# Loads of v and r behind the first inverse's operand, and a later planned start of the step that uses the inverse's result

## The chip, the core and the metric

The kernel runs on one core of a Trainium2 chip, as one program. The metric is device time in microseconds (us), the median of several runs. TensorE (PE), VectorE (DVE), ScalarE (ACT), GpSimd (POOL) and SyncE (SP) each work through their own instructions in program order. An instruction that waits holds up all that stand behind it on its engine. DMAs are issued from SP and, at a few places, from ACT, and an issue takes its turn in that engine's order too.

## The reference

A linear-attention recurrence over 768 steps, for 4 batches and 8 heads, then two feed-forward layers on the result:

```python
batch, n_heads, seq, head_dim = (4, 8, 768, 40)
for t in range(S):
    y[:, :, t] = np.einsum('bhd,bhde->bhe', rt, state)
    Sa = np.einsum('bhde,bhe->bhd', state, at)
    state_decay = state * wt[:, :, None, :] - np.einsum('bhd,bhe->bhde', Sa, bt)
    state = state_decay + np.einsum('bhd,bhe->bhde', vt, kt)
...
x = attn_out.transpose(0, 2, 1, 3).reshape(B * S, H * D)   # 3072 x 320
h = np.maximum(x @ w_in, 0.0); x = h * h @ w_out            # 320 -> 2048 -> 320
silu = g * (1.0 / (1.0 + np.exp(-g)))                       # g = x @ w_gate
out = silu * (x @ w_val) @ w_out                            # 320 -> 1536 -> 320
```

## The kernel before

**Chunks.** The 768 steps are cut into chunks of 32 (C). A unit is one chunk of two batches with all 8 heads. There are 48 units (NS), and units 2I and 2I+1 make a pair; 24 pairs follow each other in the recurrence, one waiting for the state of the last.

**Steps of a unit,** with the letter that the text uses and the line of the PE work: `e_stage` loads a, b, k, w (tile wakb, or room for two early units), scans the decays (DT) and forms AB and KB; x (L809) makes the 32x32 triangular matrix L of each head and stores it to DRAM (xi_d). For a window of 4 units, `inverse` loads the diagonal 16x16 blocks (tile xi, "the inverse's operand"), eliminates in 15 steps of two instructions each on DVE (L839, L842), and sends the result through DRAM (p_d<-xi, then p1t<-p_d). v (L868) needs p1t, p (L875) completes the inverse. Then the recurrence of a pair: u (L961, L967) needs v's values (tile TV) and the state, s (L980) applies the inverse to u, t (L1006) makes the new state. z, c, y (L1036, L1045, L1064) make the output and need the loads RB (v and r in another layout) and RH (r). The first feed-forward layer (L466, L471, tiles w1h, w1l, o1h, o1l, gh, gl; "MoE1" in the text) starts when units 0 to 3 have their y and runs between the attention's steps; its float64 weights (tile cx) are converted on ACT, DVE and POOL as they come in. Matmuls on the identity (L1299, "fillers") are put where the plan sees PE idle; their results are not used.

**What sets the order.** No order is written by hand. Every operation is handed to a planner (class `Plan`) with its engines' costs, what it reads and writes, and a due time. The planner plays the program through with these costs and issues each engine's instructions in the order that comes out. On the chip that order is fixed, and each instruction waits for what it really needs. `lag` is added to the planned arrival of what comes from a DMA:

```python
o.ready[e] = max(o.ready[e], p.done + (self.HOP[p.eng][e] + (o.lag if p.eng == SP or o.tag == "sq" else 0.0) if p.eng else 0.0))
```

**What the change touches.** `inverse` (keys of the load of xi), `stage` and the v step in `beside`, the loads of TV in `chain` and of RB and RH in `slot`. These loads may go on SP or, for the first units, on ACT (last argument of `load`). Their source lists were empty, so they could be issued as soon as their tile was free.

## Time and profile before

| what | value |
|---|---|
| three runs, median (lowest to highest) | 1197.45 us (1188.45 to 1198.04) |
| the profiled execution: its time, its span | 1193.31 us, 1191.5 us |
| PE busy | 1120.7 us, 94% |
| DVE, ACT, POOL busy | 642.9, 551.0, 97.5 us |
[...]
| y of the last unit starts | 736 us |

The first 740 us hold the attention with MoE1 between its steps, the rest of MoE1 and the second feed-forward layer follow. A row of the timeline is: start, duration, engine (with q: the engine's queue, which issues a DMA), line, operation, out<-in, shape, count, and in brackets how long the engine had been idle before it and what ended that.

### The profile page before, as it was taken

What the parts mean: (1) busy time and instruction counts of PE and PEld (TensorE: products, weight loads), DVE (VectorE), ACT (ScalarE), POOL (GpSimd) and SP (SyncE); (2) the same over time, 40 slices, a digit from 0 to 9 for tenths busy, and PEclk for the clock granted to TensorE, in tenths of its full rate; (3) what the DMA queues carried; (4) which work ended last, traced back from release to release, by engine and by line L of the source; (5) the groups of instructions that cost most, each with busy time, mean ns of one, the idle gap of its engine ahead of it and who ended that gap; (6) DMA issues with size and microseconds to landing.
All of it is one profiled execution on the core that took longest, in us unless ns stands there. A gap on an engine that the chain in (4) does not pass through costs nothing.

```text
span 1191.5 us, 43044 instructions
## 1 busy us (share of the span) xinstructions
PE 1120.7 (94%) x18634; PEld 1015.9 (85%) x18634; DVE 642.9 (54%) x1548; ACT 551.0 (46%) x1295; POOL 97.5 (8%) x122
## 2 busy tenths in 40 slices
PE   6688889999999998999999999999999999999997
PEld 5677778888989897889898899988888888888886
DVE  4776866757648573856464432455334343434433
ACT  6455876445546563655454454654223222222221
POOL 0211431101101111110000000000000000000000
PEclk9788988988999998999999999999999999999998
DMA  5754756455556564654443322432101010100000
GB/s 137 177 138 125 181 145 173 121 139 153 146 153 191 137 172 128 170 125 105 113 99 90 68 60 67 140 98 75 36 7 28 16 27 23 27 23 1 23 1 26
DMA packets 204695, 114.98 MB, mean 96 GB/s; under 512 B 104784, under 2 KB 203984, under 8 KB 204496
## 3 DMA queue, kind: packets, MB, share of 16 engines
q1 hardware_dynamic: 200867, 110.31, 36.1%
q8 instruction: 148, 2.42, 0.9%
q10 hardware_dynamic: 3629, 1.83, 0.6%
q14 instruction: 51, 0.42, 0.1%
HBM read 88.35 MB, written 23.72 MB: 94 GB/s over the span
## 4 chain that ended last, share of the span: by engine, by line
PE 69%; DMA 7%; DVE 3%; SPq 3%; issue 2%; ACT 1%; DVEq 0%; ACTq 0%
PE ps L466 32%; PE ps L471 11%; PE ps L1490 10%; SPq L730 3%; PE ps L1064 2%; PE ps L1045 2%; DMA ws<-f_moe_w_val 2%; DMA p1t<-p_d 1%; PE ps L1036 1%; PE ps L1006 1%; PE ps L967 1%; PE ps L980 1%; PE ps L868 1%; PE ps L1079 1%; PE ps L809 1%
## 5 line engine op out<-in xcount | busy, mean ns | idle before, releaser
L1482 DVE TENSOR_TENSOR gr<-ps,gr 128x512 f32<-128x512 f32 x144 | 99.5, 692 | 168.6 <-PE ps L466 85.8
L1158 ACT ACTIVATE ps<-ps 128x512 f32<-128x512 f32 x192 | 111.8, 582 | 97.6 <-PE ps L466 93.2
L471 PE MATMUL ps<-o1h,gh 128*128 128x320 f32 x384 | 132.8, 346 | 1.5 <-ACT gh L441 1.4
L441 ACT CAST gh<-gr 128x512 fp32r<-128x512 f32 x72 | 44.6, 620 | 175.7 <-DVE gr L1482 175.3
L471 PE MATMUL ps<-o1h,gl 128*128 128x320 f32 x384 | 122.8, 320 | 2.5 <-DVE gl L415 2.5
L471 PE MATMUL ps<-o1l,gh 128*128 128x320 f32 x384 | 121.5, 317 | 0.0
L466 PE MATMUL ps<-xh,w1h 128*128 128x256 f32 x384 | 115.6, 301 | 2.3 <-ACT xh L441 2.3
L466 PE MATMUL ps<-xl,w1h 128*128 128x256 f32 x384 | 109.6, 285 | 1.7 <-DVE xl L1107 1.0
L466 PE MATMUL ps<-xh,w1l 128*128 128x256 f32 x384 | 108.8, 283 | 0.3 <-DVE w1l L1239 0.3
L1490 PE MATMUL ps<-o2l,gh 128*128 128x320 f32 x288 | 88.7, 308 | 0.2 <-DVE o2l L1406 0.2
L1490 PE MATMUL ps<-o2h,gl 128*128 128x320 f32 x288 | 88.7, 308 | 0.1
L1490 PE MATMUL ps<-o2h,gh 128*128 128x320 f32 x288 | 88.7, 308 | 0.0
L415 DVE TENSOR_TENSOR gl<-ps,gh 128x512 fp32r<-128x512 f32 x96 | 65.6, 683 | 34.3 <-ACT gh L441 33.8
L1479 ACT ACTIVATE gr<-ps 128x512 f32<-128x512 f32 x72 | 43.1, 598 | 82.0 <-PE ps L466 80.3
L471 PEld LDWEIGHTS ps<-o1h,gh 128*128 128x128 f32 x384 | 75.1, 195 | 6.0 <-ACT gh L441 2.2
L471 PEld LDWEIGHTS ps<-o1h,gl 128*128 128x128 f32 x384 | 74.9, 195 | 5.8 <-DVE gl L415 5.5
L466 PEld LDWEIGHTS ps<-xh,w1h 128*128 128x128 f32 x384 | 74.1, 193 | 4.1 <-ACT xh L441 2.5
L466 PEld LDWEIGHTS ps<-xl,w1h 128*128 128x128 f32 x384 | 74.3, 193 | 2.6 <-DVE xl L1107 1.8
L471 PEld LDWEIGHTS ps<-o1l,gh 128*128 128x128 f32 x384 | 75.3, 196 | 0.1
L1139 DVE TENSOR_TENSOR gl<-gr,gh 128x512 fp32r<-128x512 f32 x72 | 49.8, 692 | 46.7 <-ACT gh L441 46.7
L466 PEld LDWEIGHTS ps<-xh,w1l 128*128 128x128 f32 x384 | 74.1, 193 | 0.5 <-DVE w1l L1239 0.5
L1299 PE MATMUL ps<-ident 128*128 128x256 f32 x296 | 51.7, 330 | 19.7 <-DVE w1l L1239 7.3
(171 smaller groups left out, 2725.2 us busy)
## 6 DMA issues: line engine op xcount, KB each, us to landing
wakb<-in_wakb_dram SPq DMA_DIRECT2D x44, 312.0 KB
RB<-in_vr_e_dram SPq DMA_DIRECT2D x45, 208.0 KB
RH<-in_r_e_dram SPq DMA_DIRECT2D x89, 80.0 KB
cx<-in_moe_w_out_dram SPq DMA_DIRECT2D x21, 320.0 KB
wakb<-in_wakb_dram SPq DMA_DIRECT2D x44, 110.5 KB
room<-xt_d SPq DMA_DIRECT2D x36, 128.0 KB
xt_d<-yb SPq DMA_DIRECT2D x24, 160.0 KB
x_d<-room SPq DMA_DIRECT2D x24, 160.0 KB
```

What stands on the lines that cost most here:

```text
L415: nc.vector.tensor_sub(dst, full, hi.bitcast(F32))
L441: nc.scalar.copy(dst, src) if e == ACT else eng[e].tensor_copy(dst, src)
L466: nc.tensor.matmul(ps, w[:, c], x, start=(i == 0), stop=(i == len(seq_) - 1))
L471: nc.tensor.matmul(acc[t][:, :DM], g[:, half, ts], w[:, f, :], start=(f == 0 and i == 0), stop=(f == nf - 1 and i == 2),)
L730: o = att(cost, lambda e: queues[e].dma_start(dst(), src()), r, w, due=due, dma=dma, tag="dma")
L1045: nc.tensor.matmul(v[64 * p:64 * p + 64, jh, u], RW[:, 4 * jh + 2 * u + p], RB[:, :, C * s:C * s + C], start=True, stop=True)
L1139: op({POOL: t_pool(512), DVE: t_dve(512)}, lambda e: eng[e].tensor_sub(gl[n], two["gr"][n], gh[n].bitcast(F32)), (("gr", n), ("gh", n)), ( ...
L1158: op({ACT: 0.478}, lambda e, f=f: nc.scalar.activation(P1[b], P1[b], f), (), (("p", b),), due=due, tag="relu")
L1299: nc.tensor.matmul(PS[:, b, 0:256].rearrange("p (a b) -> p a b", a=2), warm, warm[:, None, :].to_broadcast([128, 2, 128]), start=True, sto ...
L1479: op({ACT: 0.478}, lambda e: nc.scalar.activation(both(two["gr"]), two["pg"][b], AF.Sigmoid), (("pg", b),), (("gr", n),), tag="sig", **kw)
L1482: op({DVE: 0.602}, lambda e, q=q: nc.vector.tensor_mul(both(two["gr"]), two[q][b], both(two["gr"])), ((q, b),), (("gr", n),), tag="u" + q, ...
L1490: nc.tensor.matmul(ACC2[t][:, :DM], x[n][:, t // 2, c], y[:, f, :], start=(f == 0 and i == 0), stop=(f == nf - 1 and i == 2))
```

## The change

Three edits. (1) The load of xi gets a key ("xil", window, half), and for the first `BEHIND` = 4 units the loads of TV, RB and RH read this key of window 0: they are issued only when the first inverse's operand has landed. (2) v gets `lag` = 4.0: the plan takes v as ready 4 us later after its DMA than before. (3) RH loses the gap of 2 elements between its halves, so that its load is one row of 512 elements a partition instead of two of 256.

```diff
+LATE_V = 4.0
+BEHIND = 4
...
-    RH = ap_.tile([EPAD, 2, row], F32, name="RH")
+    RH = ap_.tile([EPAD, 2, 8 * C], F32, name="RH")
...
+    def behind(i):
+
+        return [("xil", 0, r) for r in range(2)] if i < BEHIND else ()
...
-        o = att({PE: cost}, lambda e: mm(tag), r, (tag,), due=due, take=n, tag=tag, mode=mode, act=act)
+        o = att({PE: cost}, lambda e: mm(tag), r, (tag,), due=due, take=n, tag=tag, mode=mode, act=act, lag=lag)
...
-                 [("xid", w % 2, o, p) for o in range(ns) for p in range(2)], (kx[r],), due - 1, 0.8, 0.7)
+                 [("xid", w % 2, o, p) for o in range(ns) for p in range(2)], (kx[r], ("xil", w, r)), due - 1, 0.8, 0.7)
...
-              ({ACT: 0.25}, lambda e, tag: copy(e, VT[:, :, :, 0:HC], view(tag)), ("vtz",), ("vt",)), mode="32x32", act=220)
+              ({ACT: 0.25}, lambda e, tag: copy(e, VT[:, :, :, 0:HC], view(tag)), ("vtz",), ("vt",)), mode="32x32", act=220, lag=LATE_V)
...
-                         lambda p=p, jh=jh, vsrc=vsrc: vsrc[p, jh], (), (("Tv", b, u, p, jh),), due - 0.7, 0.12, 0.62, I < SIDE)
+                         lambda p=p, jh=jh, vsrc=vsrc: vsrc[p, jh], behind(2 * I), (("Tv", b, u, p, jh),), due - 0.7, 0.12, 0.62, I < SIDE)
...
-            load(lambda p=p: RH[64 * p:64 * p + D, :, 0:8 * C], lambda: a["r_e"][data(i)].rearrange("d q s t -> d q (s t)"), (), (("Rr", p),), due + 0.3, 0.23, 0.0, i < 2 * SIDE)
+            load(lambda p=p: RH[64 * p:64 * p + D].rearrange("d q t -> d (q t)"), lambda: a["r_e"][data(i)].rearrange("d q s t -> d (q s t)"), behind(i), (("Rr", p),), due + 0.3, 0.23, 0.0, i < 2 * SIDE)
```

The load of RB changes as that of TV does. Since the planner's order hangs together, the order changes on every engine up to the end of the attention. Three places follow. Line numbers of the changed kernel are higher by 2 to 6.

**The first inverse's operand, on SP.** xi_d<-L0 to L3 are the stores of the first four triangular matrices, xi<-xi_d the load of the operand. Before:

```order
L730 DMA xi_d0_60<-L0_121 32x256 x2
L730 DMA TV0_157<-in_v_t_dram 32x4x40 x4
L730 DMA xi_d0_60<-L1_122 32x256 x2
L730 DMA RB_164<-in_vr_e_dram 104x2x256
L730 DMA xi_d0_60<-L2_123 32x256 x2
L730 DMA RH_160<-in_r_e_dram 40x2x256
L730 DMA TV1_158<-in_v_t_dram 32x4x40 x4
L730 DMA xi_d0_60<-L3_124 32x256 x2
L1254 DMA cx0_114<-in_moe_w_in_dram 128x2x128
L1254 DMA cx1_115<-in_moe_w_in_dram 128x2x128
L1254 DMA cx2_116<-in_moe_w_in_dram 64x2x128 x2
L730 DMA xi_169<-xi_d0_60 64x16x16 x2
```

Now, from the second store on (the loads of cx0, cx1 and cx2 have moved ahead of it):

```order
L732 DMA xi_d0_60<-L1_122 32x256 x2
L732 DMA xi_d0_60<-L2_123 32x256 x2
L732 DMA wakb0_166<-in_wakb_dram 104x272
L732 DMA wakb0_166<-in_wakb_dram 104x3x256
L732 DMA wakb1_167<-in_wakb_dram 104x272
L732 DMA wakb1_167<-in_wakb_dram 104x3x256
L732 DMA xi_d0_60<-L3_124 32x256 x2
L1260 DMA cx0_114<-in_moe_w_out_dram 128x2x160
L732 DMA room_106<-in_wakb_dram 104x272
L732 DMA room_106<-in_wakb_dram 104x3x256
L732 DMA xi_169<-xi_d0_60 64x16x16 x2
```

The loads of TV, RB and RH are gone from between the stores, and the loads of wakb for units 4, 5 and 6 stand there instead.

**The first inverse's result, on ACT.** xi<-qt (the copy that hands over the result) and UQ<-ps (u's result) are L441 before and L443 now. Before:

```order
L1217 ACTIVATE cx0_114<-cx0_114 128x2x160
L1219 ACTIVATE ps_113<-cx0_114 128x320
L441 COPY xi_169<-qt_170 64x256
L441 CAST w1hl_103<-ct2_119 64x256 x3
L441 COPY ps_113<-ct2_119 64x256
```

Now:

```order
L742 ACTIVATE sq_168,stat_76<-DT5_141 104x256
L732 DMA TV0_157<-in_v_t_dram 32x4x40 x4
L732 DMA RB_164<-in_vr_e_dram 104x2x256
L732 DMA RH_160<-in_r_e_dram 40x512
L732 DMA TV1_158<-in_v_t_dram 32x4x40 x4
L742 ACTIVATE sq_168,stat_76<-wakb1_167 104x256
L1223 ACTIVATE cx1_115<-cx1_115 128x2x128
L1225 ACTIVATE ps_113<-cx1_115 128x256
L443 COPY UQ_159<-ps_113 128x320
L443 COPY xi_169<-qt_170 64x256
```

The issue of ten loads and the copy of u's result now stand ahead of the copy of the inverse's result.

**The second inverse, on DVE.** ut<-ps and ST<-ut end a t step, tmp<-qt,xi 128x15 is the first instruction of an inverse. Before:

```order
L1009 TENSOR_TENSOR ut_165<-ps_113,ST0_151 104x320
L1048 TENSOR_TENSOR RC_161<-ps_113,mask_177 128x256
L1018 TENSOR_TENSOR ST0_151<-ut_165,DT2_138 104x2x4x40
L839 TENSOR_TENSOR tmp_171<-qt_170,xi_169 128x15
L1009 TENSOR_TENSOR ut_165<-ps_113,ST1_152 104x320
L1239 TENSOR_TENSOR o1l_105<-ps_113,o1h_104 128x320
L1018 TENSOR_TENSOR ST1_152<-ut_165,DT3_139 104x2x4x40
L842 TENSOR_TENSOR qt_170<-qt_170,tmp_171 128x15
```

Now:

```order
L1015 TENSOR_TENSOR ut_165<-ps_113,ST0_151 104x320
L1024 TENSOR_TENSOR ST0_151<-ut_165,DT0_136 104x2x4x40
L1015 TENSOR_TENSOR ut_165<-ps_113,ST1_152 104x320
L1024 TENSOR_TENSOR ST1_152<-ut_165,DT1_137 104x2x4x40
L845 TENSOR_TENSOR tmp_171<-qt_170,xi_169 128x15
L848 TENSOR_TENSOR qt_170<-qt_170,tmp_171 128x15
```

DT2 and DT3 belong to the second pair, DT0 and DT1 to the first: the second inverse began inside the second pair's t and now begins behind the first pair's.

## Rows read from the trace of the kernel before

**Rows 1.** Window: us, busy (instructions) of PE, PEld, DVE, ACT, POOL, granted clock, DMA share

```profile
300.00:400.00 100.00, 96.96 (x2520) 89.65 (x2521) 67.72 (x191) 58.26 (x143) 14.46 (x16) 1.00 0.59 155
```

**Rows 2.** Timeline of SP's queue, 20 to 46 us

```profile
20.95 0.90 SPq L730 DMA_DIRECT2D RH<-in_r_e_dram  x1
21.96 3.33 SPq L730 DMA_DIRECT2D TV<-in_v_t_dram  x4
25.39 1.00 SPq L730 DMA_DIRECT2D xi_d<-L  x2
...
28.88 1.35 SPq L730 DMA_DIRECT2D xi<-xi_d  x2
...
41.27 0.62 SPq L730 DMA_DIRECT2D p_d<-xi  x1
...
44.95 0.80 SPq L730 DMA_DIRECT2D p1t<-p_d  x2
```

**Rows 3.** Timeline of DVE, 19 to 52 us

```profile
19.23 0.42 DVE L812 TENSOR_TENSOR L<-ps,mask 128x256 f32<-128x256 f32 x1 [0.79 <-PE ps L809]
30.50 0.43 DVE L1221 TENSOR_SCALAR ps<-ps 128x256 int32<-128x256 int32 x1 [10.85 <-ACT ps L1219]
...
33.12 0.18 DVE L839 TENSOR_TENSOR tmp<-qt,xi 128x15 f32<-128x15 f32 x1 [0.84 <-DMA xi<-xi_d]
...
40.34 0.18 DVE L842 TENSOR_TENSOR qt<-qt,tmp 128x15 f32<-128x15 f32 x1
...
51.39 0.41 DVE L812 TENSOR_TENSOR L<-ps,mask 128x256 f32<-128x256 f32 x1
```

**Rows 4.** Timeline of ACT and its queue, 12 to 41 us

```profile
12.19 0.61 ACTq L730 DMA_DIRECT2D TV<-in_v_t_dram  x1
...
15.78 4.30 ACTq L730 DMA_DIRECT2D TV<-in_v_t_dram  x4
20.19 0.42 ACT L740 ACTIVATE sq<-DT 104x256 bf16<-104x256 f32 x1 [4.09 <-DMA TV<-in_v_t_dram]
...
40.55 0.63 ACT L441 COPY xi<-qt 64x256 f32<-64x256 f32 x1 [1.14 <-DVE qt L842]
```

**Rows 5.** Timeline of PE, 50 to 115 us

```profile
50.20 1.05 PE L868 MATMUL ps<-p1t,L 32*32 32x16 f32 x64
...
56.08 1.20 PE L980 MATMUL ps<-UQ,P 32*32 32x40 f32 x57
...
59.41 1.31 PE L1006 MATMUL ps<-TV,KT 64*40 64x40 f32 x64
...
78.14 0.83 PE L1006 MATMUL ps<-TV,KT 64*40 64x40 f32 x64
...
93.77 0.28 PE L1064 MATMUL ps<-RH,SX 40*40 40x32 f32 x8
...
108.95 0.39 PE L466 MATMUL ps<-xh,w1h 128*128 128x256 f32 x1
...
114.86 0.76 PE L980 MATMUL ps<-UQ,P 32*32 32x40 f32 x62
```

**Rows 6.** Timeline of DVE, 82 to 196 us

```profile
82.04 0.17 DVE L839 TENSOR_TENSOR tmp<-qt,xi 128x15 f32<-128x15 f32 x1
...
96.46 0.18 DVE L842 TENSOR_TENSOR qt<-qt,tmp 128x15 f32<-128x15 f32 x1
...
195.56 0.49 DVE L1239 TENSOR_TENSOR o1l<-ps,o1h 128x320 fp32r<-128x320 f32 x1 [0.50 <-ACT ps L441]
```

**Rows 7.** Groups by line, PE: busy, mean ns of one, idle before it and what ended it

```profile
L1299 PE MATMUL ps<-ident 128*128 128x256 f32 x296 | 51.7, 330 | 19.7 <-DVE w1l L1239 7.3 <-ACT ident L441 6.6 <-DVE ct L1224 3.2
L1064 PE MATMUL ps<-RH,SX 40*40 40x32 f32 x1536 | 36.6, 202 | 3.4 <-DMA RH<-in_r_e_dram 2.6 <-DVE ut L1009 0.5
...
L868 PE MATMUL ps<-p1t,L 32*32 32x16 f32 x1536 | 21.7, 185 | 10.9 <-DMA p1t<-p_d 8.4 <-issue 2.2
...
L875 PE MATMUL ps<-P,vt 32*32 32x16 f32 x1536 | 19.5, 183 | 2.2 <-issue 1.7 <-DMA P<-pt_d 0.4
```

## The prediction

> **What bounds the kernel now.** I read the windows first. From 300 us on PE is the bound: 96.96 of 100 us busy at a granted clock of 1.00 [rows 1]. Then I compared the orders of the two programs. In both, 352 matmuls of MoE1 stand ahead of the twelfth unit's y and 2356 ahead of the last one, so from the twelfth y on the same work remains at the same points. A lasting gain or loss is made before that, in the first 230 us, or in waits of PE later. So the early stretch is read closest, engine by engine.

> There a chain decides. On SP's queue the stores of the first four L stand between loads of v and r: the second four of TV take 3.33 us, one RH 0.90 us, and the last store is issued at 25.39 although its L was ready at 19.65 (19.23 + 0.42) [rows 2, 3]. DVE idles 10.85 us and starts the first inverse at 33.12, when its operand has landed [rows 3]. Its result comes back as p1t, v runs at 50.20, s of the first pair at 56.08, t at 59.41, and MoE1 starts at 108.95, 15.2 us behind the start of the fourth y at 93.77 [rows 5]. The third s, which needs the second inverse, comes only at 114.86, after MoE1's start [rows 5].

> **The change part by part.** The base is the profiled execution, 1193.3 us, with a span of 1191.5. It is 4.1 us under the median shown (1197.45) and inside the three runs.

> *A. From the first operand to the first s.* The loads leave the gaps between the stores, but others move in. On SP the last store now stands behind three weight loads and four loads of wakb, on DVE its L stands behind the first weight's conversion, and the inverse behind the scans of units 4 and 5 and conversions. ACT no longer issues TV before its squares. It was free at 16.10 (20.19 less 4.09) [rows 4]; seven squares at some 0.55 us and two conversions bring the first converted weight to DVE at about 20.8. The block of DVE that now stands ahead of the inverse is nearly what stood behind it before, from 40.52 (40.34 + 0.18) to 51.80 (51.39 + 0.41), 11.3 us [rows 3]. So the inverse starts at 20.8 + 11.3 = 32.1, 1.0 us sooner than 33.12. The operand is not the later one: L is ready at about 22, and last store to operand took 33.12 - 25.39 = 7.7 us [rows 2, 3], which gives 29.7. That is the low end (-3.4); 33.1, if the wakb loads hold the small pieces up, is the high end.

> The inverse ends 7.4 us later, at 39.5 against 40.52 [rows 3]. On ACT ten issues of loads, two conversions, a square and the copy of u's result stand now ahead of the copy of the inverse's result. One issue takes 0.61 us while SP issues little and 4.30 / 4 = 1.08 us beside SP's own TV loads [rows 4]. SP has nine at the same time (2 x 3.33 + 0.90 = 7.6 us [rows 2]), so I take the dear one: from 29.7 to 40.5, and the copy is over at about 43 where it was over at 41.18 (40.55 + 0.63) [rows 4]. Behind it stand p_d<-xi and p1t (41.27, 44.95 before [rows 2]). On PE 30 filler matmuls, 30 x 51.7 / 296 = 5.2 us [rows 7], stand now ahead of v. Out of this s of the first pair comes later, not sooner: between -1 and +5 us, I take **+2.5**.

> [...]

> *B. The second inverse.* This is where the gain is. It moves on DVE from inside the second pair's t to right behind the first pair's t. That t was at 59.41 [rows 5], now about 62; the inverse can start at 64 where it started at 82.04 [rows 6]. It lasted 14.5 us with other work between (82.04 to 96.64), and from its end to the third s went 18.2 us [rows 5, 6]: 64 + 14.5 + 18.2 = 97 instead of 114.86. In the new order the third s, its t and the fifth y stand ahead of MoE1's first matmul. MoE1 still needs the fourth y plus 15.2 us, so its start moves by 0 to -5. What lasts is PE work of a pair that leaves the crowded time behind 109 us for a time of fillers and waits. A pair costs 14.9 us of PE: thirteen groups from the L1064 row to the L875 row, 357.0 us in all, over 24 pairs [rows 7]. Not all of the pair moves (its u stood ahead before, half of its y's stand behind still). Ends: 0 (see the first rival) and 14.9 + 5 = 19.9; I take **-9**, some three fifths of a pair and no earlier start.

> *C. v later in the plan.* PE waited 8.4 us for p1t at v's head, and 2.2 us are put down to issue there [rows 7]. With v 4 us later in the plan other matmuls stand in those places. Ends: 0, if s, t and y wait instead, and -8.4; I take half, **-4**, since from 300 us on there is enough MoE1 work to stand in between.

> *D. Fillers.* 304 instead of 296: 8 x 0.175 = **+1.4** [rows 7].

> *E. RH.* The layout may shorten an issue of 0.90 us [rows 2], but with as many partitions it need not. PE waited 2.6 us for RH in all [rows 7]. Ends 0 and -2.6; I take 0, since SP's queue shows as bound in none of the rows behind 60 us that I use.

> Sum: 2.5 - 9 - 4 + 1.4 = -9.1, **1184 us**, which is 1.1% under the median shown. About 1% is what a measurement of this kernel can tell from no change.

> **The rivals.**

> *Absorbed.* Between 109 and 196 us MoE1 runs no faster than its weights are converted; the last one is at 195.56 [rows 6]. If that paces the stretch, a third s that is ready sooner changes nothing, B is 0, C some -2, and A is eaten by the same slack: 1193.3 + 0 - 2 + 1.4 = 1193. For it: the new order has converted no more weights at the third s than the old. Against it: DVE and ACT still have waits there, and the moved pair's DVE work leaves that stretch too.

> *Slower.* The loads of v and r now come too late. Their burst starts when the operand lands, and the result's copy waits on ACT behind the burst and behind u, which needs TV. If the operand lands at 33 as before instead of 29.7, the burst ends at 33 + 10.8 = 43.8 and the copy at 46, 5 us late; the fillers ahead of v come on top (5.2), less the 1 to 2 us by which PE would have idled. Up to MoE1's start all is chain, so +8 would last: 1193.3 + 8 + 1.4 = 1203. It decides from the point where the operand lands after about 31 us. For it: 2 wakb pairs are queued ahead of the operand. Against it: DMA engines are not full in that time before.

> [...]

> *Larger.* B and C at their far ends: 1193.3 + 2.5 - 19.9 - 8.4 + 1.4 = 1169. It needs MoE1 to start 5 us sooner and PE to be the only bound behind it.

> **How the numbers follow.** Forecast 0.53 (own range 1177 to 1192), absorbed 0.22 (1189 to 1198), slower 0.15 (1197 to 1212), larger 0.10 (1165 to 1177). The range reaches from the middle of the larger case to the middle of the slower one, 1171 to 1205, and leaves out about 2 in 10. Faster by over 1% means under 1185.5: somewhat over half of the forecast's case and the larger one whole, less a little for my reading of A, 0.42. Slower by over 1% means over 1209.4: the upper third of the slower case and other mishaps, 0.10. Within 1%: 0.48.

> **What would show it.** In the new profile: first inverse on DVE at 31 to 33 us (not under 29); the copy xi<-qt at about 42; s of the first pair at 57 to 61; the second inverse at 62 to 67; the third s before the first MoE1 matmul, at 95 to 102; the idle time of v on p1t halved; the last y of the attention some 9 us ahead of 736. I am wrong if the third s is early and the last y is not (absorbed), or if the first s is later than 62 (slower).

## The result and the profile after

| what | before | changed |
|---|---|---|
| median of the runs | 1194.78 us (4 runs, 1188.45 to 1198.04) | 1209.60 us (4 runs, 1201.29 to 1217.62) |
| ratio, 95% interval | | **1.0132 [1.0086, 1.0178]** |
| profiled execution, its span | 1193.31, 1191.5 us | 1212.11, 1210.3 us |
| PE busy; idle | 1120.7; 70.8 us | 1127.3; 83.0 us |
| its mean granted TensorE clock, as a share | 0.963 | 0.957 |
| y of the last unit starts | 736 us | 750.5 us |

The change costs 1.3%. The forecast was 1184 us, 9.1 us (0.8%) under its base of 1193.3; 1209.6 us lies above the forecast's whole range, 1171 to 1205. Of the 18.8 us between the two spans, 15.5 are there when MoE1 ends and 15.7 at the last matmul; 3.1 lie behind it, in the stores of the output.

First the early chain. SP's queue in the changed kernel, 25 to 49 us (start, duration), the rows that answer to [rows 2]:

```profile
25.25 1.32 SPq L732 DMA_DIRECT2D xi<-xi_d  x2
...
33.00 3.28 SPq L732 DMA_DIRECT2D TV<-in_v_t_dram  x4
36.32 0.52 SPq L732 DMA_DIRECT2D RH<-in_r_e_dram  x1
...
41.76 0.61 SPq L732 DMA_DIRECT2D p_d<-xi  x1
42.42 2.02 SPq L732 DMA_DIRECT2D pt_d<-qt  x1
44.95 1.67 SPq L732 DMA_DIRECT2D xi_d<-L  x2
...
48.04 0.77 SPq L732 DMA_DIRECT2D p1t<-p_d  x2
```

ACT and its queue, for [rows 4]:

```profile
28.32 0.74 ACTq L732 DMA_DIRECT2D TV<-in_v_t_dram  x1
29.09 1.91 ACTq L732 DMA_DIRECT2D TV<-in_v_t_dram  x3
31.03 0.80 ACTq L732 DMA_DIRECT2D RB<-in_vr_e_dram  x1
31.92 0.30 ACTq L732 DMA_DIRECT2D RH<-in_r_e_dram  x1
33.16 3.12 ACTq L732 DMA_DIRECT2D TV<-in_v_t_dram  x4
...
39.69 0.64 ACT L443 COPY xi<-qt 64x256 f32<-64x256 f32 x1
```

The operand's load goes out 3.6 us sooner, and the result's copy starts 0.9 us sooner. But p1t is issued 3.1 us later than before, mostly since other issues have moved between p_d and p1t. DVE, for [rows 3, 6], first instruction of the first and of the second inverse:

```profile
30.53 0.17 DVE L845 TENSOR_TENSOR tmp<-qt,xi 128x15 f32<-128x15 f32 x1
...
70.13 0.17 DVE L845 TENSOR_TENSOR tmp<-qt,xi 128x15 f32<-128x15 f32 x1
```

PE, for [rows 5]: first v, first s, third s, first matmul of MoE1:

```profile
53.36 0.87 PE L874 MATMUL ps<-p1t,L 32*32 32x16 f32 x64 [3.95 <-DMA P<-pt_d]
...
63.34 0.89 PE L986 MATMUL ps<-UQ,P 32*32 32x40 f32 x40
...
108.53 1.02 PE L986 MATMUL ps<-UQ,P 32*32 32x40 f32 x48
...
125.77 0.39 PE L468 MATMUL ps<-xh,w1h 128*128 128x256 f32 x1
```

The second inverse is 11.9 us sooner and the third s stands ahead of MoE1, as the order said, but the first s is 7.3 us and MoE1 16.8 us later. Yet against the kernel before this is not where most of the time stays lost. The twelfth y, ahead of which the same matmuls of MoE1 stand, starts 3.3 us later than before (234.1 and 230.8 us), the 32nd 2.8 us sooner (527.2 and 530.0, but with 40 fewer matmuls of MoE1 ahead of it, some 6 us at the 0.147 us that lie between the starts of two), and the 44th, from which on the two orders of PE are the same, 14.8 us later (709.1 and 694.3). Two windows of that stretch, for [rows 1], and the second one in the kernel before (us, busy of PE, PEld, DVE, ACT, POOL, granted clock):

```profile
300.00:400.00 100.00, 89.35 (x2343) 82.31 (x2344) 57.86 (x163) 47.96 (x122) 8.46 (x10) 0.90 0.53 140
...
530.00:600.00 70.00, 66.84 (x1721) 62.19 (x1720) 36.03 (x100) 33.66 (x82) 4.61 (x7) 0.95 0.48 121
```

```profile
530.00:600.00 70.00, 68.60 (x1816) 63.63 (x1816) 39.46 (x106) 35.49 (x85) 2.05 (x3) 1.00 0.47 113
```

Where PE was busy for 96.96 of 100 us at full clock, it is now for 89.35 at 0.90, and for 66.84 us at 0.95 where it was 68.60 at 1.00. The groups by line, for [rows 7], and u's group in the kernel before (L961 there):

```profile
L1305 PE MATMUL ps<-ident 128*128 128x256 f32 x304 | 54.5, 333 | 10.9 <-ACT ident L443 6.6 <-DVE ct L1230 3.6 <-DVE w1hl L1245 0.7
...
L967 PE MATMUL ps<-TV,L 32*32 32x40 f32 x1536 | 22.5, 205 | 10.6 <-issue 7.1 <-DMA TV<-in_v_t_dram 3.4
...
L881 PE MATMUL ps<-P,vt 32*32 32x16 f32 x1536 | 20.2, 185 | 8.8 <-issue 8.2 <-ACT vt L443 0.5
L874 PE MATMUL ps<-p1t,L 32*32 32x16 f32 x1536 | 19.7, 183 | 7.0 <-DMA P<-pt_d 3.9 <-issue 2.8 <-ACT TV L996 0.2
```

```profile
L961 PE MATMUL ps<-TV,L 32*32 32x40 f32 x1536 | 20.8, 204 | 1.8 <-issue 1.7
```

At v (L874) the 8.4 us for p1t are gone. At p (L881) 2.2 us of idle time have become 8.8, and at u (L967) 1.8 have become 10.6, most of it put down to issue, time in which PE waits for nothing that the profile names. One such place, PE's timeline:

```profile
368.07 0.68 PE L881 MATMUL ps<-P,vt 32*32 32x16 f32 x62
...
368.61 0.76 PE L967 MATMUL ps<-TV,L 32*32 32x40 f32 x61
373.15 0.22 PE L967 MATMUL ps<-TV,L 32*32 32x40 f32 x1 [3.78 <-issue]
```

PE stops in the middle of one u, between two matmuls of the same tiles. The DMA queues in just this gap, 369.2 to 373.3 us (packets, MB, share):

```profile
q1 hardware_dynamic: 1059, 0.74, 73.2%
q8 instruction: 1, 0.02, 1.6%
```

The one packet on q8, the queue that the profile calls instruction, runs in the trace from 370.68 to 371.70, and PE goes on 1.4 us after it has landed, at 373.15. Counting PE's instructions in the trace, 26 of 27 waits of over 0.3 us that end 1.0 to 1.75 us after such a packet has landed stand at one and the same place in every 256 instructions. These 27 sum to 31.2 us; in the kernel before it is 22 waits, 19.3 us, 16 of them at that place. The trace has 148 such packets for 37,284 matmuls and weight loads on PE, 252 a packet. A packet is 16,384 bytes, two of them never start less than 3.18 us apart in this trace (3.26 in that of before), and 256 instructions (128 short matmuls and their weight loads, at 0.68 us for 62) are used up in 1.4 us. That such a packet holds PE's next 256 instructions, and that PE waits for it there, is the author's estimate from these counts and times; no row shows what a packet holds.

During the stall the clock falls (window, busy, clock; from 371.2 to 378.0 the granted share is 0.50):

```profile
364.00:371.00 7.00, 5.11 (x255) 4.76 (x256) 1.97 (x4) 2.94 (x8) 0.00 (x0) 1.00 0.68 172
371.00:378.00 7.00, 4.85 (x104) 4.26 (x107) 4.04 (x9) 0.83 (x3) 0.00 (x0) 0.51 0.36 90
```

### The profile page after: what moved, and what is told of

Its sections match the earlier page's. It is cut to its first block, busy times and chain, and to the rows that moved or that the text cites. A ratio compares the mean times of both kernels' runs of the same rounds, so it can differ in the third digit from the quotient of the medians.

```text
span 1210.3 us, 43042 instructions
## 1 busy us (share of the span) xinstructions
PE 1127.3 (93%) x18642; PEld 1021.9 (84%) x18642; DVE 645.2 (53%) x1556; ACT 548.6 (45%) x1293; POOL 95.1 (8%) x116
## 4 chain that ended last, share of the span: by engine, by line
PE 71%; DMA 4%; DVE 4%; issue 3%; ACT 1%; SPq 1%; DVEq 0%; ACTq 0%
PE ps L468 31%; PE ps L473 12%; PE ps L1496 10%; PE ps L1070 3%; PE ps L973 2%; PE ps L1051 2%; DMA ws<-f_moe_w_val 2%; PE ps L1042 1%; PE ps L1085 1%; PE ps L967 1%; PE ps L986 1%; DMA ws<-f_moe_w_gate 1%; SPq L732 1%; PE ps L815 1%; PE ps L931 1%
## 5 line engine op out<-in xcount | busy, mean ns | idle before, releaser
L443 ACT CAST gh<-gr 128x512 fp32r<-128x512 f32 x72 | 44.6, 620 | 175.4 <-DVE gr L1488 175.1
L1305 PE MATMUL ps<-ident 128*128 128x256 f32 x304 | 54.5, 333 | 10.9 <-ACT ident L443 6.6
```

What stands on the lines that cost most here:

```text
L443: nc.scalar.copy(dst, src) if e == ACT else eng[e].tensor_copy(dst, src)
L1305: nc.tensor.matmul(PS[:, b, 0:256].rearrange("p (a b) -> p a b", a=2), warm, warm[:, None, :].to_broadcast([128, 2, 128]), start=True, sto ...
```

## The experiments

Theories at the start: **early** (the loss is made in the first 130 us), **late v** (the second edit makes it, behind 300 us), **instructions** (the time goes with PE's waits for instructions, whatever edit draws the order anew). Short matmuls are those of v, p, u, s, t and y (62 of p in 0.68 us); MoE1's and the fillers are wide. The expectations price a block of 256 instructions by what its matmul time in the planned order lacks to 3.6 us; only one in twenty packets starts less than 3.5 to 3.6 us after the one before it in the traces of before and of the change. Three numbers are read from each run. The ratio is to the kernel before on the same chip. "Clock" is span x (1 - mean granted clock), averaged over the kernel's executions, less the same for the kernel before in the same call; that one lay between 36.0 and 41.6 us. "p1t" and "issue" are PE's waits for p1t and those put down to issue between 130 and 720 us, all lines together, of the profiled execution. That is one execution of each kernel, which lies up to 17 us from the kernel's median.

| kernel | ratio [95%] | clock, us | p1t | issue |
|---|---|---|---|---|
| before | 1 | 0 | 7.5 | 10.8 |
| loads alone | 1.0035 [1.0000, 1.0070] | +5.1 | 3.8 | 7.9 |
| late v alone | 1.0321 [1.0275, 1.0366] | +25.3 | 0 | 24.0 |
| layout of RH alone | 0.9908 [0.9874, 0.9942] | -3.7 | 4.9 | 12.5 |
| loads and layout | 0.9908 [0.9880, 0.9936] | -4.1 | 4.2 | 9.2 |
| all three (the change) | 1.0132 [1.0086, 1.0178] | 52 in all | 0 | 24.0 |

**One edit at a time.** The kernel before with one edit each, and the change with the second edit doubled:

```diff
# loads alone: LATE_V = 0.0, old RH      # late v alone: BEHIND = 0, old RH
-    RH = ap_.tile([EPAD, 2, row], F32, name="RH")         # layout alone
+    RH = ap_.tile([EPAD, 2, 8 * C], F32, name="RH")
-LATE_V = 4.0                                               # doubled
+LATE_V = 8.0
```

Loads alone. 

> The kernel before with the first edit alone: the loads of TV, RB and RH of the first four units wait for the first inverse's operand; v keeps its plan, RH its old layout. Early theory (the loss is made in the first 130 us, where the first s came 7.2 us and MoE1's start 16.8 us later than before): 1203 to 1212 us, ratio 1.008 to 1.015, first MoE1 matmul near 126 us. Late-v theory (the loss is made between 300 and 700 us by v's later place in the plan): within 4 us of before, 1191 to 1199. Instruction theory (PE loses its time where short matmuls stand so close that its instructions don't come in fast enough, 19.3 us of such waits in the trace of before and 31.4 in that of the changed kernel): the time goes with the sum of those waits, whichever edit changes the order.

Late v alone. 

> The kernel before with the second edit alone: v is planned 4 us later everywhere; the first loads and RH as before. Early theory: first MoE1 matmul near 109 to 112 us and within 4 us of before, 1191 to 1199. Late-v theory: 1203 to 1212 us, with the idle time of PE behind 300 us at 20 to 25 us instead of 15. Instruction theory: by the sum of PE's waits for instructions again, above 25 us if the time is over 1203, below 22 if it is under 1197.

Layout alone. 

> The kernel before with the third edit alone: RH in one row a partition. The order of PE's instructions is the same as before. All theories: within 2.6 us of before (what PE waited for RH in all), ratio 0.997 to 1.001; issue of one early RH 0.3 to 0.5 us instead of 0.9.

Doubled. 

> The changed kernel with v planned 8 us later instead of 4 (double the second edit). Late-v theory: the loss doubles, 1218 to 1230 us. Early theory: like the changed kernel, 1203 to 1213. Instruction theory: neither; the time goes with the sum of PE's waits for instructions, which a new order draws anew, somewhere from 1195 to 1215.

The early theory falls for the loads: with the loads alone MoE1 starts at 107.4 us, the third s at 106.1, and the time is that of before plus 0 to 0.7%. Late v alone costs 3.2%, more than the whole change and 19 us above the 1212 us that was the most expected, and carries the exchange of waits. The doubled edit gives 1.0150 [1.0090, 1.0209], issue 28.1, clock +9.1: not double. The layout misses every expectation: 11.5 us faster, with SP's order unchanged. The tile view of RH shows what became cheaper; the loads of RH on SP before and with the layout alone (min/median/max in ns):

```profile
L730 SPq DMA_DIRECT2D RH<-in_r_e_dram x89: 763/807/1853, 21.0 to 728.3; - x89
```

```profile
L730 SPq DMA_DIRECT2D RH<-in_r_e_dram x89: 281/309/1857, 21.0 to 716.7; - x89
```

Half a microsecond less 89 times; all issues on SP together last 569.6 us instead of 612.6. What is queued behind an RH can go out sooner, and PE's waits for p1t fall from 7.5 to 4.9 us. How this becomes 11.5 us isn't shown: in the two profiled executions PE's idle time is nearly the same (70.8 and 70.2 us), and its busy time is 9.7 us less (1120.7 and 1111.0). The clock column has 3.7 us. The y matmuls that read RH didn't get faster (median 199 ns in both).

**The change without its second edit, a fix, and the price of instructions.** In the second kernel (spread) the planner holds a step of short matmuls back while too many PE instructions would start within 4 us. In the other two, in the order of before, v does its matmuls twice, or six fillers stand ahead of v: about equal PE time by the plan (16.3 and 16.6 us), 3072 and 288 instructions.

```diff
-LATE_V = 4.0                                               # late v undone
+LATE_V = 0.0
+WORDS = {"v": 128, "p": 128, "u": 192, "s": 128, "t": 128, "x": 32, "k": 8, "z": 8, "c": 32, "y": 128, "S": 8}
+SUPPLY = 4.0, 320
+    def dense(self, o, t):                                  # spread
+        return self.words(o) + sum(n for x, n in self.sent[-60:] if x > t - SUPPLY[0]) > SUPPLY[1]
+                if not o.cols and self.dense(o, t):
+                    return False
-            for u in range(2):                             # doubled v
+            for u in (0, 0, 1, 1):
+            for _ in range(3):                             # fillers ahead of v
+                plan.filler(plan.bank(tag))
```

Late v undone. 

> The changed kernel with the second edit undone (v planned as before); the loads behind the operand and the new layout of RH stay. If the parts add, 1195.6 - 11.5 (the layout alone) + 4.4 (the loads alone) = 1188 us, and the late v is what costs the changed kernel some 21 us. If the parts act only together, it stays near 1209. If the gain of the layout was the luck of one placement, 1196 to 1202.

Spread. 

> The changed kernel, in which the planner also leaves out a step of short matmuls as long as more than 320 PE instructions would start within 4 us, and takes MoE1 matmuls first. Instruction theory: what blocks of 256 instructions lack to 3.6 us of matmul time, summed over the order, falls from 81 us to 64 (before: 69), so PE waits less for instructions, the clock falls less often, and the time is 1192 to 1203 us. Late-v theory in its plain form (v stands too late for the steps behind it, whatever stands between): 1205 to 1215.

Doubled v. 

> The kernel before in which each v does its matmuls twice (the same result): 24 x 64 short matmuls more in the same order, at 0.68 us per 64 that is 16.3 us of PE time and 12 blocks of instructions. If only PE time counts: 1195.6 + 16 = 1212 us at most. Instruction theory: the sum of what the blocks lack rises from 69 to 99 us, a third to all of that 30 comes on top, and the clock falls more often: 1222 to 1245, PE's waits for instructions 30 us or more.

Fillers. 

> The kernel before with six filler matmuls ahead of each v: 24 x 6 x 0.115 = 16.6 us of PE time, the same as in the kernel with doubled v, in 288 instructions instead of 3072. If only PE time counts: the same time as with doubled v, 1212. Instruction theory: the sum of what the blocks lack falls from 69 to 59 us: 1203 to 1212, at least 12 us below the doubled v, PE's waits for instructions under 19 us.

Without the late v the ratio is 0.9908: edits 1 and 3 add within the intervals (0.9943 by their two ratios), and the second edit costs 1.0132 / 0.9908, 2.3%. Beside this kernel the change is 11.7 us late at the twelfth y already (234.1 and 222.4 us, with 12 more MoE1 matmuls ahead of it, some 2 us) and 27.8 us at the 44th (709.1 and 681.3). So about a third of what the second edit costs is made in the first 230 us; the comparison with the kernel before hid it, since the kernel with edits 1 and 3 is 8.4 us ahead there.

Doubled v gives 1.0394 [1.0340, 1.0449], 47.5 us more, fillers 1.0041 [1.0002, 1.0080], 4.6 us more, for about the same PE work in the same order. Of the 43 us between them 32 are clock (+23.1 against -9.0). v's group in the kernel with v doubled, and with the fillers:

```profile
L868 PE MATMUL ps<-p1t,L 32*32 32x16 f32 x3072 | 37.9, 185 | 22.5 <-issue 15.9 <-DMA p1t<-p_d 5.2 <-ACT SX L441 1.3
```

```profile
L870 PE MATMUL ps<-p1t,L 32*32 32x16 f32 x1536 | 18.9, 181 | 2.1 <-DMA p1t<-p_d 1.3 <-issue 0.6
```

The fillers' waits for issue are 10.3 us between 130 and 720, about as before (10.8); with v doubled they are 28.5. The 3072 instructions more bring 12 more packets on q8 (160 and 148). Not all of the difference need lie in the kind of matmul: the fillers also fill time in which PE waited for p1t (8.4 us at v before, 1.3 with them). So more short matmuls in a row were dear here far beyond their PE time: 47.5 us for some 16, with 17.7 us more of waits for issue and 23.1 us more lost by the clock. But the spread order of the changed kernel, in which waits for issue fell from 24.0 to 18.0, gained nothing: 1.0124 [1.0073, 1.0176], clock +10.7. The instruction theory in its plain form falls too.

**Where the late v costs, and what holds the clock.** v late up to unit 15 alone, from unit 16 on alone; fillers ahead of each v in the changed kernel, and two instead of six with late v undone:

```diff
-              ... mode="32x32", act=220, lag=LATE_V)
+              ... mode="32x32", act=220, lag=LATE_V if g < 16 else 0.0)   # head; tail: g >= 16
+            for _ in range(3):                             # fillers; range(1) with LATE_V = 0.0
+                plan.filler(plan.bank(tag))
```

Head. 

> The changed kernel with v planned later for the first 16 units alone (to some 290 us); the rest as with the second edit undone. If the harm of the late v is made behind 300 us, where the clock falls for 27 to 48 us with it and 10 to 14 without: ratio to before 0.990 to 0.998. If it is made early, in the crowded time up to 300 us: 1.005 to 1.015, near the changed kernel.

Tail. 

> The changed kernel with v planned later from unit 16 on alone. If the harm is made behind 300 us: ratio 1.004 to 1.013, half the clock for 25 us or more behind 300 us, PE's waits put down to issue behind 300 us above 10 us. If it is made early: 0.989 to 0.996, like the kernel with the second edit undone.

Fillers on the change. 

> The changed kernel with six filler matmuls ahead of each v (16.6 us of PE work in 288 instructions), in the same order. On the kernel before they cost 4.6 us, since the clock gave 9 us back. Clock theory (most of the changed kernel's loss is time at half clock, 52 us lost against 38): they give back more here, up to 24 us, so the time is that of the changed kernel less 0 to 7 us, ratio 1.005 to 1.013. If its loss is waits for data that a longer run of PE doesn't hide: the changed kernel plus 5 to 17 us, ratio 1.017 to 1.027.

Two fillers, late v undone. 

> The changed kernel with the second edit undone and two filler matmuls ahead of each v, 5.5 us of PE work. If fillers there hold the clock as they did on the kernel before (9 us back for 16.6 us put in, waits for p1t shorter by some us): between 5 us faster and 2 us slower than without them, ratio to before 0.986 to 0.993. If the kernel with the layout alone has little left to give back: 0.993 to 0.996.

Head 1.0066 [1.0033, 1.0099], tail 1.0028 [0.9998, 1.0057], against 0.9908 with neither: both halves cost, 1.6% and 1.2%. The tail's ratio lies under the 1.004 to 1.013 expected for harm made behind 300 us, and each of the two is also an order drawn anew, which alone can cost as much (see below). The first s is at 61.9 us with the head alone and at 56.2 with the tail alone, so the late first s of the change is the late v's doing, not the loads'. The tail shows the exchange most cleanly. PE's waits behind 300 us with late v undone (us, times, longest):

```profile
PE ps L874 <- DMA p1t<-p_d: 4.2, 6, 1.5
PE ps L1051 <- issue: 1.5, 1, 1.5
PE ps L874 <- issue: 1.3, 1, 1.3
```

and with v late from unit 16 on:

```profile
PE ps L1070 <- issue: 6.4, 3, 3.7
PE ps L986 <- issue: 3.8, 4, 1.7
PE ps L881 <- issue: 2.2, 1, 2.2
PE ps L973 <- issue: 1.9, 1, 1.9
```

No wait for p1t is left, and issue goes from 4.8 to 18.6 us, now at y, s, p and u inside the run of short steps; clock from -4.1 to +6.7. Six fillers on the change give 1.0151 [1.0105, 1.0196]: of 16.6 us put in, some 14 come back, against 12 on the kernel before. The interval reaches into both expected ranges (up to 1.013 by the clock, from 1.017 by waits for data), so this run doesn't decide between them. Two fillers with late v undone give 0.9936 [0.9908, 0.9965]: nothing left to gain there.

**Is it the late v, or any new order?** With late v undone: v 0.1 us later, p or c planned 0.02 or 0.01 us dearer (all without meaning), v 2 us earlier.

```diff
+LATE_V = 0.1                                               # or -2.0
-        stage("p", g, 0.54, p_mm,
+        stage("p", g, 0.56, p_mm,
-        stage("c", i, 0.47, c_mm,
+        stage("c", i, 0.48, c_mm,
```

A tenth. 

> The changed kernel with v planned 0.1 us later instead of 4: next to nothing, but the planner draws the order anew (473 lines of PE's order differ from those without it). If the later place of v is what costs: ratio 0.988 to 0.996, like the kernel without it. If any order drawn anew is worse than the one there was: 1.003 to 1.015.

p. 

> The changed kernel with the second edit undone and p planned at 0.56 us instead of 0.54, a change without meaning that draws the order anew (579 lines of PE's order differ). If the later place of v is what costs: ratio 0.988 to 0.998. If any order drawn anew is worse: 1.003 to 1.015.

c. 

> The changed kernel with the second edit undone and c planned at 0.48 us instead of 0.47, a change without meaning that draws the order anew (512 lines differ). If the later place of v is what costs: ratio 0.988 to 0.998. If any order drawn anew is worse: 1.003 to 1.015.

Early. 

> The changed kernel with v planned 2 us earlier instead of 4 later. If the later place of v is what costs, the other direction brings waits for p1t back (above 6 us between 130 and 720 us) and waits for instructions stay near 9 us: ratio 0.988 to 1.000. If any order drawn anew is worse: 1.003 to 1.015 with waits for instructions of 15 us or more.

| kernel | ratio [95%] | clock, us | p1t | issue |
|---|---|---|---|---|
| v 0.1 us later | 0.9926 [0.9891, 0.9961] | -2.6 | 0.2 | 17.9 |
| p at 0.56 | 1.0046 [1.0010, 1.0082] | +4.4 | 1.7 | 21.9 |
| c at 0.48 | 0.9991 [0.9958, 1.0025] | -2.9 | 1.8 | 19.4 |
| v 2 us earlier | 1.0170 [1.0108, 1.0232] | +7.5 | 19.0 | 17.8 |

A new order alone costs 0.2, 1.4 and 0.8% against 0.9908, and it too brings issue to some 20 us. The first lies in the range expected if the place of v is what costs, the second in the one for any new order, the third between the two. v moved by 2 us or more in either direction costs 2.3 to 2.6%. The early one lies above both of its expected ranges; its waits are those for p1t, as its group shows:

```profile
L874 PE MATMUL ps<-p1t,L 32*32 32x16 f32 x1536 | 21.3, 185 | 25.9 <-DMA p1t<-p_d 23.1 <-issue 1.3 <-DVE DT L787 1.1
```

The profiled executions tell the two theories apart up to the twelfth y. It stands at 213.8 to 225.9 us in the eight kernels (none spread) with the loads moved and v at most 0.1 us late up to unit 15, the neutral orders among them, with 340 MoE1 matmuls ahead of it. With the loads moved and v late from the start, and none spread, it stands at 233.9 to 245.1 us in four kernels, with 352 ahead of it (380 in the doubled one, where 40 more are some 6 us). So in that stretch it is the late v that costs. From the twelfth y to the 44th the change takes 475.0 us, the kernel with loads and layout 458.9, and the three neutral orders 458.3, 473.3 and 466.2: there an order drawn anew can lose as much. Late v alone takes 480.4 there, against 463.5 before.

**Spreading where v is not late.** The planner that spreads, on the layout alone, and on loads and layout (diff as above, LATE_V = 0.0; BEHIND = 0 in the first).

Layout, spread. 

> The kernel before with the layout of RH and a planner that holds a step of short matmuls back while more than 320 PE instructions would start within 4 us; no edit 1, no late v. What the blocks of 256 instructions lack to 3.6 us falls from 69 to 48 us over the order. If instructions are a cause of their own: waits put down to issue below 9 us between 130 and 720 us and a ratio of 0.970 to 0.988, under the 0.991 of the layout alone. If a redrawn order costs its 0 to 1.4% whatever its density: 0.991 to 1.005.

Loads and layout, spread. 

> The changed kernel with the second edit undone and the same planner that spreads the short matmuls; the sum of what blocks lack goes from 71 to 57 us. If instructions are a cause of their own: ratio 0.975 to 0.990. If a redrawn order costs its 0 to 1.4%: 0.991 to 1.005.

0.9978 [0.9947, 1.0010] with issue at 7.0 us, and 0.9963 [0.9935, 0.9991] with 12.1. The waits for instructions shrink in one of them to the lowest of all these orders, and the time is 0.7 and 0.6% above the same edits unspread. Each of these is a new order too, so that what spreading itself does stays unseparated from what a new order costs. Waits for instructions in an order are thus no measure of its time by themselves.

## Why the prediction was wrong

**The step that failed is C.** It took "v 4 us later in the plan other matmuls stand in those places" at -4 us, with 0 as its bad end, "if s, t and y wait instead". The waits for p1t went as it said (7.5 to 0 us behind 130 us). But the bad end was too good: the second edit costs 2.3% beside the others, some 27 us, and 3.2% alone. The waits of the steps behind v are longer than the one removed (issue from 10.8 to 24.0 us), they lie inside the runs of short matmuls, and at half clock 52 us are lost where it was 36 to 42; the sum has no term for the clock. Ahead of the twelfth y the late v makes a part of the loss, with the first s at 61.8 us where it is late and nothing else is changed. For the rest, three neutral orders cost 0.2 to 1.4% and four kernels with v late throughout 2.2 to 3.2%, which speaks for the place of v; with three draws it isn't shown that a neutral order can't lose as much.

**E was mis-sized.** RH was taken at 0 with an end of -2.6, because SP's queue showed as bound in no row used. It is 11.5 us (0.9%): the row of 0.90 us was the price of one of 89 loads on SP, whose queue's issues together became 43 us shorter. By which path this reaches PE wasn't isolated.

**A** (+2.5, between -1 and +5) was right in size where v is not late: the first s at 56.9 and 57.8 us against 56.1. In the changed kernel it is at 63.3, 7.3 us later, by the late v. The burst on ACT was priced too dear, at 10.8 us; it lasted 8.0 (28.32 to 36.28). The row of 4.30 us behind that price was misread: it lies at 15.78 to 20.08, and SP's own TV loads beside it end at 16.70, so most of it stands beside stores of L. The cheaper price, 6.1 us for ten at the 0.61 us an issue of [rows 4], was the nearer one.

**B** was right in place and wrong in size. In the changed kernel, with the loads alone and with loads and layout the second inverse starts at 70.1 to 71.9 us (forecast 62 to 67) and the third s at 106.1 to 108.5, ahead of MoE1 (forecast 95 to 102), and with the loads alone the fifth y comes 8 us sooner. But the loads alone cost 0 to 0.7%, and beside the layout nothing: in its outcome the rival named absorbed holds for B. Its reason, the pace of the weights up to 196 us, isn't shown: at the 20th y, ahead of which the same MoE1 matmuls stand, the traces still have a lead of 3.3 us with the loads alone (352.5 and 355.8) and 4.4 us beside the layout (345.8 and 350.2). Where the lead goes was not isolated. The slower rival's sign, a first s later than 62 us, came true, but not its mechanism (the loads too late): with the loads alone and with loads and layout the first s comes at most 1.7 us later than before. Its 1203 came nearest to the 1209.6, by another cause.

**D** counted 8 more fillers rightly at +1.4 us; their group is 2.8 us busier (51.7 and 54.5 us). The premise that a lasting gain or loss is made in the first 230 us "or in waits of PE later" left out the clock, and only the first of these two places was worked out: against the kernel before, the twelfth y, at 231 us, was 3.3 us late, the 44th 14.8. Two slips change nothing: 82.04 to 96.64 is 14.6 us, not 14.5, and by the prediction's own chances its range leaves out some 0.13, not 0.2.

The best version of these is the layout of RH, alone or with the loads moved, 0.9908 of before. **Open stays** why an order with v late throughout loses more clock than the neutral new orders (+9 to +25 us against -3 to +4; +4.5 and +6.7 with v late in the head and in the tail alone), when its waits for instructions are only some 2 to 10 us longer, and no longer in the spread order (18.0 us) and with the head alone (15.8). That spreading, fillers and a smaller or larger lag didn't give the time back shows only that none of these alone is the cause.

## What to carry to other kernels

A wait at the head of a run of short matmuls was not lost time alone here: in the tail kernel, where the 4.2 us for p1t behind 300 us were taken away, the waits put down to issue grew from 4.8 to 18.6 us, and those at y, s, p and u stood inside the runs; by which path was not shown. Compare two orders at points ahead of which the same work stands, and each edit with the kernel that lacks it alone, else one edit's gain hides another's loss. Before an edit to a planner is judged by its aim, draw the order anew a few times by changes without meaning, since the spread (here 0.2 to 1.4%) is as large as most effects looked for. Price what a DMA issue costs the queue over the whole program: a contiguous row in place of two, 0.5 us 89 times on SP, was worth more here than anything done to the order.
